# Attention scores in 64-row by 32-column tiles of the array instead of 64 by 64

## The chip, the cores and the metric

The kernel runs on one core of one Trainium2 chip. The metric is the device time of one execution in microseconds (us); the time of a kernel is the median of its runs.

## The reference

A sliding-window attention with linear position biases, followed by a two-layer block with a hard-swish in between. Batch 8, 8 heads, 576 positions, 64 numbers a head; 4608 tokens of width 512, inner width 2048.

```
scores = (1/sqrt(64)) * q @ k.T                       # per batch and head, 576 x 576
mask   = (rel >= 0) & (rel < 128)                     # rel = query position - key position
scores = where(mask, scores - slope[h] * abs(rel), -1e9)
attn   = softmax(scores)
x      = (attn @ v), heads side by side               # 4608 x 512
h      = x @ w_in
out    = (h * clip(h + 3, 0, 6) / 6) @ w_out
```

A query sees itself and the 127 keys before it. Seen from a key at place p of a block of 128 keys, the queries that can see it are those at places p to p + 127, counted from the block's start.

## The kernel before, in words

The order of the instructions on every engine is written out by hand (a manual schedule), and each engine works through its own in that order. The work is 32 groups `g`, one for each batch and pair of heads (head `e` is 0 or 1, and sits in rows 64e to 64e + 63 of the transposed queries `qT` and keys `kT`). Batches 0 and 1 have code of their own (`first_batch`, `second_batch`); from batch 2 on, `segment` takes one group after the other. In each turn it has, for group `g`: `scores` (matmuls of keys and queries), `exp_diag` and `exp_off` (exponentials on ScalarE, then a triangular mask on GpSimd), and for group `g - 1` `values` (the matmuls with v and the division) and `back` (the way into `xT`, from which the second part reads). Between these stand calls of `fill`, each of which puts one unit of the two-layer block there: four matmuls with 512 columns, by `moe_up` (L502) or `moe_down` (L552).

The scores of a group stand in two tiles `sce`, one for each head: 128 keys of a block in the partitions, and for each of four key blocks `j` 256 queries, as `s` = 0 (the queries of the same block, read by `exp_diag`) and `s` = 1 (those of the next block, read by `exp_off`). The fifth block has only 64 keys and 64 queries; its scores go into a corner of block 3 that is otherwise free (L373), read through `p4buf`. The first group with this layout, `g` = 8, is computed by `scores_whole` over whole blocks and fills both tiles; the groups after it, 9 to 31, use the loop at L359 to L374. It cuts a key block into two halves of 64 keys (`half`, first key `lo`), and for each half takes only 192 queries from `lo` on, since no other query sees any of these keys. A matmul there uses 64 rows of the array (one head's 64 numbers) and 64 columns (64 keys), a quarter of it; head and half give four such quarters. Places of `sce` that are not written keep older scores, and the masks after the exponentials (L406, L415, L421) put zeros there.

Of the kernel before, what the change touches and what calls it, by code (L numbers as in the profile page):

```python
# [18 lines left out]
def kernel(  # L19
# [9 lines left out]
    nc = tc.nc  # L29
    B, H, S, D = q.shape  # L30
# [7 lines left out]
    LAST = S - 4 * 128  # L38
# [222 lines left out]
    def full(g):  # L261
        return g < NB_FULL * NP
# [12 lines left out]
    def rooms(g):  # L275
        b, hp = divmod(g, NP)
        if full(g):
            room = w_out_sb if b == 0 else gbuf[1]
            for i, nm in enumerate(("pd", "po")):
                st[g, nm] = room[:, ds(4 * hp + 2 * i, 2), :].rearrange(  # L280
                    "p e (j c) -> p e j c", j=4)
        else:
            st[g, "pd"] = ppool.tile([128, 2, 4, 128], BF16, tag="pd", name="pd")
            st[g, "po"] = ppool.tile([128, 2, 4, 128], BF16, tag="po", name="po")

    def scores_diag(g):
        rooms(g)
        b, hp = divmod(g, NP)
        qT, kT = qTb[b % 2][:, hp, :, :], kTb[b % 2][:, hp, :, :]
        first = not diag_tabled(g)  # L290
        if (g, "scd") not in st:
            tables_diag(g)
        scd = st[g, "scd"]
        for j in range(4):
            for e in range(2):
                r = slice(e * D, (e + 1) * D)
                nc.tensor.matmul(scd[:, e, ts(j, 128)], lhsT=kT[r, j, :],
                                 rhs=qT[r, j, :], start=first, stop=first or j == 3)
# [15 lines left out]
    def scores_off(g):  # L314
        b, hp = divmod(g, NP)
        qT, kT = qTb[b % 2][:, hp, :, :], kTb[b % 2][:, hp, :, :]
        foff = not full(g)
        if (g, "sco") not in st:
            tables_off(g)
        sco = st[g, "sco"]  # L320
        for e in range(2):
            r = slice(e * D, (e + 1) * D)
            nc.tensor.matmul(sco[:, e, 64:128], lhsT=kT[r, 4, :],
                             rhs=qT[r, 4, 0:LAST], start=foff, stop=foff)
        for j in range(4):
            n = 128 if j < 3 else LAST
            for e in range(2):
                r = slice(e * D, (e + 1) * D)
                nc.tensor.matmul(sco[:, e, ds((j + 1) % 4 * 128, n)], lhsT=kT[r, j, :],
                                 rhs=qT[r, j + 1, 0:n], start=foff, stop=foff or j == 3)  # L330
    def scores_whole(kT, qT, sce):
        for j in range(4):
            for e in range(2):
                r = slice(e * D, (e + 1) * D)
                n = min(256, S - 128 * j)
                nc.tensor.matmul(
                    sce[e][:, j, :, :].rearrange("p s c -> p (s c)")[:, 0:n],
                    lhsT=kT[r, j, :], rhs=qT[r, ds(128 * j, n)], start=True, stop=True)
        for e in range(2):
            r = slice(e * D, (e + 1) * D)  # L340
            nc.tensor.matmul(sce[e][:, 3, 1, 64:128], lhsT=kT[r, 4, :], rhs=qT[r, 512:S],
                             start=True, stop=True)

    def scores(g):
        if full(g):
            scores_diag(g)
            scores_off(g)
            return
        rooms(g)
        b, hp = divmod(g, NP)  # L350
        qT = qTb[b % 2][:, hp, :, :].rearrange("p j c -> p (j c)")
        kT = kTb[b % 2][:, hp, :, :]
        if g == 2 * NP:
            st["sce"] = [ps_sc.tile([128, 4, 2, 128], FP32, tag="sc", name="sce")
                         for _ in range(2)]
            scores_whole(kT, qT, st["sce"])
            return
        sce = st["sce"]
        for j in range(4):  # L359
            for half in range(2):  # L360
                lo = 64 * half
                n = min(192, S - 128 * j - lo)
                for e in range(2):
                    r = slice(e * D, (e + 1) * D)
                    nc.tensor.matmul(  # L365
                        sce[e][lo:lo + 64, j, :, :].rearrange("p s c -> p (s c)")[:, ds(lo, n)],
                        lhsT=kT[r, j, lo:lo + 64], rhs=qT[r, ds(128 * j + lo, n)],
                        start=True, stop=True)
        for half in range(2):
            lo = 64 * half  # L370
            for e in range(2):
                r = slice(e * D, (e + 1) * D)
                nc.tensor.matmul(sce[e][lo:lo + 64, 3, 1, 64:128], lhsT=kT[r, 4, lo:lo + 64],  # L373
                                 rhs=qT[r, 512:S], start=True, stop=True)  # L374

    def exp_off_full(g):
        nc.scalar.activation(out=st[g, "po"].rearrange("p e j c -> p e (j c)"),  # L377
# [290 lines left out]
    def second_batch():  # L668
# [12 lines left out]
        for i in range(4):  # L681
            load_w_out(i)
        g = 2 * NP - 1
        scores(g)
        exp_diag(g, 0)
        exp_diag(g, 1)
# [25 lines left out]
        done[0] = 2 * NP  # L712
        fill(2)
        scores(2 * NP)

    FILLS = {g: (1, 1, 1, 2, 0, 1, 1) for g in (9, 10, 11, 13, 14, 15)}

    def segment(lo, hi, fills):
        for g in range(lo, hi + 1):
# [3 lines left out]
            if lo < g < hi and g != 3 * NP + 1:  # L723
                scores(g)
# [88 lines left out]
```

## Time and profile before

| | before |
|---|---|
| time, median of 3 runs (lowest, highest) | 322.15 us (321.69, 322.75) |
| span of the profiled execution | 319.2 us |
| busy time of TensorE / weight loads | 310.1 / 164.9 us |
| busy time of ScalarE, VectorE, GpSimd | 195.7, 173.1, 141.2 us |
| score matmuls with 192 or 128 columns (L365) | 368, busy 11.9 us |
| score matmuls of the fifth block (L373) | 92 |

The time of a run covers a little more than the span, which goes from the first to the last instruction of the program. PE is TensorE, PEld its weight loads, ACT ScalarE, DVE VectorE, POOL GpSimd. "64*64 64x192" in a row is the tile of the array that a matmul uses, and then partitions by columns of what it reads. Matmuls run one into the other: the duration that the profile gives to one holds its way through the array, so that the distance from start to start tells what it costs in a series, and a busy TensorE may still be waiting in part.

### The profile page before, as it was taken

To read this page: it belongs to the slowest core of one execution; us is meant where nothing else is said; L and a number is where in the kernel's file an instruction comes from. 1 tells how busy PE (TensorE), PEld (TensorE's weight loads), DVE (VectorE), ACT (ScalarE), POOL (GpSimd) and SP (SyncE) were. 2 spreads that over 40 slices of the span, in tenths; PEclk is the share of its full clock that TensorE was granted. 3 is DMA by queue.
4 is the path that set the end of the run, shared out by engine and by line. 5 is a ranking of instruction groups with operands and counts; after the bars stand their busy time and mean duration, and the time that the engine had idled before them with its cause. 6 is when DMAs were issued, how large, how long until landed. Compare 5 with 4: busy or idle time off the path is not lost.

```text
span 319.2 us, 7124 instructions
## 1 busy us (share of the span) xinstructions
PE 310.1 (97%) x2775; PEld 164.9 (52%) x2775; DVE 173.1 (54%) x338; ACT 195.7 (61%) x334; POOL 141.2 (44%) x249
## 2 busy tenths in 40 slices
PE   7879999999999999999999999999999999999996
PEld 5565465455545454445677654444444444444443
DVE  6667675554355655655565556555656455455510
ACT  4748976877767776676676667666764344244401
POOL 8464493684496477266744673663331000000000
PEclk9999999999999999999999999999999999999999
DMA  7999999999999999998999999962212110000112
GB/s 281 199 323 225 256 260 195 249 231 194 215 252 157 239 208 211 205 222 194 207 205 211 209 190 196 225 93 68 38 39 88 53 36 33 33 33 35 66 56 75
DMA packets 131425, 51.90 MB, mean 163 GB/s; under 512 B 118976, under 2 KB 123328, under 8 KB 131392
## 3 DMA queue, kind: packets, MB, share of 16 engines
q1 hardware_dynamic: 126160, 45.36, 68.0%
q0 software_dynamic: 4224, 4.19, 8.2%
q10 hardware_dynamic: 1008, 1.90, 1.6%
q8 instruction: 21, 0.34, 0.5%
q14 instruction: 12, 0.10, 0.1%
HBM read 36.70 MB, written 9.44 MB: 145 GB/s over the span
## 4 chain that ended last, share of the span: by engine, by line
PE 86%; DMA 5%; ACT 4%; POOL 2%; DVE 2%; issue 1%; POOLq 0%
PE ops L552 38%; PE hps L502 36%; DMA w_in_sb<-in_moe_w_in_dram 3%; PE sce L365 3%; PE av L442 2%; PE av L434 2%; DMA ldbuf<-in_k_dram 2%; ACT r L521 2%; PE ops L533 1%; ACT kTb L245 1%; ACT gbuf L399 1%; PE tp L243 1%; DVE gbuf L522 0%; ACT gbuf L377 0%; PE tb L483 0%
## 5 line engine op out<-in xcount | busy, mean ns | idle before, releaser
L522 DVE SCALAR_TENSOR_TENSOR gbuf<-r,hps 128x512 bf16<-128x512 f32 x144 | 98.7, 688 | 101.0 <-ACT r L521 99.8
L521 ACT ACTIVATE r<-hps,bias 128x512 f32<-128x512 f32 x144 | 98.9, 689 | 86.8 <-PE hps L502 86.6
L502 PE MATMUL hps<-xT,w_in_sb 128*128 128x512 bf16 (+1 forms) x640 | 144.9, 358 | 0.6 <-ACT xT L489 0.3
L552 PE MATMUL ops<-w_out_sb,gbuf 128*128 128x512 bf16 x560 | 137.8, 379 | 0.0
L502 PEld LDWEIGHTS <-w_in_sb 128*128 128x128 bf16 x640 | 59.3, 98 | 55.0 <-issue 0.8
L552 PEld LDWEIGHTS <-gbuf 128*128 128x128 bf16 x560 | 51.9, 98 | 56.3
L415 POOL TENSOR_SCALAR_AFFINE_SELECT po<-po 128x512 bf16<-128x512 bf16 x48 | 30.3, 636 | 32.5 <-ACT po L413 32.4
L406 POOL TENSOR_SCALAR_AFFINE_SELECT pd<-pd 128x512 bf16<-128x512 bf16 x48 | 29.8, 634 | 33.5 <-ACT pd L389 33.5
L389 ACT ACTIVATE pd<-sce,bias_d 128x512 bf16<-128x512 f32 x48 | 31.7, 684 | 5.4 <-PE sce L373 2.7
L561 DVE COPY osb<-ops 128x512 f32<-128x512 f32 x33 | 22.7, 688 | 20.0 <-PE ops L552 17.5
L195 POOL CAST tbuf<-ldbuf 128x512 bf16<-128x512 f32 (+1 forms) x45 | 25.6, 614 | 16.8 <-issue 9.3
L413 ACT ACTIVATE po<-sce,bias_o 128x512 bf16<-128x512 f32 x48 | 33.0, 687 | 0.0
L453 DVE TENSOR_TENSOR avs<-av,rc 128x384 bf16<-128x384 f32 (+1 forms) x48 | 23.6, 491 | 1.6
L442 PEld LDWEIGHTS <-pd 128*128 128x128 bf16 x192 | 14.3, 97 | 8.3 <-issue 0.5
L434 PE MATMUL av<-vbuf,po 128*128 128x65 bf16 x192 | 18.0, 193 | 0.0
L442 PE MATMUL av<-vbuf,pd 128*128 128x65 bf16 x192 | 17.3, 193 | 0.3 <-ACT kTb L245 0.3
L434 PEld LDWEIGHTS <-po 128*128 128x128 bf16 x192 | 14.3, 98 | 2.9 <-DVE avs L453 0.5
L188 POOL CAST vbuf<-ldbuf 128x1024 bf16<-128x1024 f32 x14 | 14.2, 1043 | 3.5 <-DMA ldbuf<-in_v_dram 3.5
L418 ACT ACTIVATE p4buf<-sce,bias_d 128x64 bf16<-128x64 f32 x48 | 15.5, 323 | 0.0
L228 POOL CAST pr<-ldbuf 128x576 bf16<-128x576 f32 x20 | 12.9, 670 | 5.1 <-DMA ldbuf<-in_k_dram 3.1
L365 PE MATMUL sce<-qTb,kTb 64*64 64x192 bf16 (+1 forms) x368 | 11.9, 245 | 0.0
L365 PEld LDWEIGHTS <-kTb 64*64 64x64 bf16 x368 | 7.1, 106 | 8.6 <-issue 8.5
(104 smaller groups left out, 208.4 us busy)
## 6 DMA issues: line engine op xcount, KB each, us to landing
out_dram<-osb SPq DMA_DIRECT2D x33, 256.0 KB, 2.5
ldbuf<-in_v_dram SPq DMA_DIRECT2D x32, 256.0 KB, 5.2
ldbuf<-in_q_dram SPq DMA_DIRECT2D x20, 256.0 KB, 5.3
ldbuf<-in_k_dram SPq DMA_DIRECT2D x16, 256.0 KB, 4.4
ldbuf<-in_q_dram SPq DMA_DIRECT2D x12, 288.0 KB, 7.0
ldbuf<-in_k_dram SPq DMA_DIRECT2D x12, 288.0 KB, 6.3
w_in_sb<-in_moe_w_in_dram POOLq DMA_DIRECT2D x4, 512.0 KB, 9.2
w_out_sb<-in_moe_w_out_dram POOLq DMA_DIRECT2D x4, 512.0 KB, 10.3
```

The source lines that it names most:

```text
L195: nc.gpsimd.tensor_copy(out=tbuf[:m, :, j, :], in_=s[:m, j, :, :].rearrange("p (i e) d -> p i (e d)", e=2))
L365: nc.tensor.matmul(sce[e][lo:lo + 64, j, :, :].rearrange("p s c -> p (s c)")[:, ds(lo, n)], lhsT=kT[r, j, lo:lo + 64], rhs=qT[r, ds(128 * ...
L389: nc.scalar.activation(out=pd[:, e, :, :], in_=st["sce"][e][:, :, 0, :], func=ACT.Exp, bias=bias_d[:, h:h + 1], scale=scale)
L406: nc.gpsimd.affine_select(out=pd[:, e, :, :], in_=pd[:, e, :, :], pattern=[[0, 4], [1, 128]], channel_multiplier=-1, base=0, compare_op=AL ...
L413: nc.scalar.activation(out=po[:, e, :, :], in_=sc[:, :, 1, :], func=ACT.Exp, bias=bias_o[:, h:h + 1], scale=scale)
L415: nc.gpsimd.affine_select(out=po[:, e, :, :], in_=po[:, e, :, :], pattern=[[0, 4], [-1, 128]], channel_multiplier=1, base=-1, compare_op=A ...
L434: nc.tensor.matmul(out_av, lhsT=po[:, e, qt % 4 if full(g) else qt - 1, :], rhs=vb[:, qt - 1, h, :], start=True, stop=False)
L442: nc.tensor.matmul(out_av, lhsT=d, rhs=vb[:, qt, h, :], start=(qt == 0), stop=True)
L502: nc.tensor.matmul(hps[:, lo:hi], lhsT=w_in_sb[:, ks, ts(ms, 128)], rhs=xT[:, ks, ds(src, hi - lo)], start=(ks == 0), stop=(ks == n_ks - 1))
L521: nc.scalar.activation(out=r6, in_=hps, func=ACT.Relu, bias=bias3[:, 0:1], scale=1.0 / 6.0)
L522: nc.vector.scalar_tensor_tensor(out=gts[nt][:, ms, :], in0=r6, scalar=1.0, in1=hps, op0=ALU.min, op1=ALU.mult)
L552: nc.tensor.matmul(ops[nt, sub], lhsT=gts[nt][:, ms, ts(sub, 128)], rhs=w_out_sb[:, ms, :], start=(ms == 0), stop=(ms == n_ms - 1))
```

## The change

The loop over halves becomes a loop over eighths of the array: each key block is cut into four groups of 32 keys, and each group takes 160 queries from its first key on. In the fifth block, two groups of 32 keys cover the 64 keys (before, two halves of 64 rows covered these and 64 rows of padding), and each takes the queries from its first key on. Sizes of `sce`, the exponentials, the masks and everything else stay.

```
         for j in range(4):
-            for half in range(2):
-                lo = 64 * half
-                n = min(192, S - 128 * j - lo)
+            for lo in range(0, 128, 32):
+                n = min(160, S - 128 * j - lo)
                 for e in range(2):
                     r = slice(e * D, (e + 1) * D)
                     nc.tensor.matmul(
-                        sce[e][lo:lo + 64, j, :, :].rearrange("p s c -> p (s c)")[:, ds(lo, n)],
-                        lhsT=kT[r, j, lo:lo + 64], rhs=qT[r, ds(128 * j + lo, n)],
+                        sce[e][lo:lo + 32, j, :, :].rearrange("p s c -> p (s c)")[:, ds(lo, n)],
+                        lhsT=kT[r, j, lo:lo + 32], rhs=qT[r, ds(128 * j + lo, n)],
                         start=True, stop=True)
-        for half in range(2):
-            lo = 64 * half
+        for lo in range(0, LAST, 32):
             for e in range(2):
                 r = slice(e * D, (e + 1) * D)
-                nc.tensor.matmul(sce[e][lo:lo + 64, 3, 1, 64:128], lhsT=kT[r, 4, lo:lo + 64],
-                                 rhs=qT[r, 512:S], start=True, stop=True)
+                nc.tensor.matmul(sce[e][lo:lo + 32, 3, 1, 64 + lo:128],
+                                 lhsT=kT[r, 4, lo:lo + 32], rhs=qT[r, 512 + lo:S],
+                                 start=True, stop=True)
```

## The prediction, made before the changed kernel ran

> **What bounds the kernel now.** I read the page first (busy shares and the chain of waits), then the stretches by stage, then who waited for whom while the changed code runs, then the timeline of one score section with its rows by line.
>
> ```profile
> PE 310.1 (97%) x2775; PEld 164.9 (52%) x2775; DVE 173.1 (54%) x338; ACT 195.7 (61%) x334; POOL 141.2 (44%) x249
> ...
> PE 86%; DMA 5%; ACT 4%; POOL 2%; DVE 2%; issue 1%; POOLq 0%
> PE ops L552 38%; PE hps L502 36%; DMA w_in_sb<-in_moe_w_in_dram 3%; PE sce L365 3%; PE av L442 2%; PE av L434 2%; DMA ldbuf<-in_k_dram 2%; ACT r L521 2%; PE ops L533 1%; ACT kTb L245 1%; ACT gbuf L399 1%; PE tp L243 1%; DVE gbuf L522 0%; ACT gbuf L377 0%; PE tb L483 0%
> ```
>
> TensorE is busy 97% of the span and carries 86% of the chain; the score matmuls of the changed loop (line 365) are themselves 3% of it. No other engine is over 61%. The stretches by stage show whether TensorE ever waits where the changed code stands:
>
> ```profile
> 61.00:89.00 28.00, 27.64 (x275) 14.50 (x275) 14.05 (x29) 21.13 (x40) 18.03 (x31) 1.00 1.08 221
> 89.00:105.00 16.00, 15.77 (x148) 8.08 (x149) 9.20 (x19) 11.49 (x21) 13.16 (x24) 1.00 1.11 208
> 105.00:145.00 40.00, 40.00 (x368) 19.89 (x366) 23.19 (x46) 27.38 (x51) 23.20 (x41) 1.00 1.13 212
> 145.00:185.00 40.00, 40.00 (x410) 25.85 (x402) 22.77 (x45) 26.78 (x50) 23.78 (x43) 1.00 1.10 209
> 185.00:234.00 49.00, 49.00 (x443) 24.50 (x443) 27.40 (x55) 32.59 (x60) 23.84 (x43) 1.00 0.69 130
> ```
>
> The columns are length, then busy time of PE, PEld, DVE, ACT and POOL, granted clock, DMA share and GB/s. From 105 to 234 us TensorE is busy all of the time at the full granted clock (1.00); before that it has 0.36 + 0.23 = 0.59 us of idle time. The changed lines run only in this part:
>
> ```profile
> L365 PEld LDWEIGHTS <-kTb x368: 102/106/107, 61.1 to 233.4; 64*64 64x64 bf16 x184
> L365 PE MATMUL sce<-qTb,kTb x368: 216/243/267, 61.1 to 233.5; 64*64 64x192 bf16 x161, 64*64 64x128 bf16 x23
> L373 PE MATMUL sce<-qTb,kTb x92: 189/189/189, 61.5 to 233.5; 64*64 64x64 bf16 x92
> ```
>
> There are 368 / 16 = 23 sections, from 61.1 to 233.5 us. Whatever a section gets shorter or longer moves everything behind it on an engine that is always busy, so the question is only how long one section is. Here is one, with the big matmuls around it. The rows between the first and the last are the same matmuls asked for in later and later narrow stretches, so that the count shows how many have started:
>
> ```profile
> 112.19 0.38 PE L502 MATMUL hps<-xT,w_in_sb 128*128 128x512 bf16 x1
> 112.50 0.28 PE L365 MATMUL sce<-qTb,kTb 64*64 64x192 bf16 x4
> 112.50 0.36 PE L365 MATMUL sce<-qTb,kTb 64*64 64x192 bf16 x8
> 112.50 0.44 PE L365 MATMUL sce<-qTb,kTb 64*64 64x192 bf16 x12
> 112.50 0.52 PE L365 MATMUL sce<-qTb,kTb 64*64 64x192 bf16 x16
> 112.83 0.21 PE L373 MATMUL sce<-qTb,kTb 64*64 64x64 bf16 x4
> 112.97 1.04 PE L552 MATMUL ops<-w_out_sb,gbuf 128*128 128x512 bf16 x4
> 113.85 1.03 PE L502 MATMUL hps<-xT,w_in_sb 128*128 128x512 bf16 x4
> ```
>
> Three things are to be seen. The matmuls come in waves of four (two heads by two halves of the keys), one wave for each of the four key blocks: the union grows 0.28, 0.36, 0.44, 0.52, that is 0.08 us a wave. Within a wave the four run beside each other: the first wave's union is 0.28 with single matmuls of 0.267, so all four started within some 13 ns. And the section costs 0.47 us from its first start (112.50) to the next big matmul (112.97); big matmuls follow each other every (113.85 - 112.97) / 4 = 0.22 us, and the section starts 0.31 us after the last one, so 0.09 us more goes in draining before it. At its end the last narrow matmul starts at 112.83 + 0.21 - 0.19 = 112.85.
>
> **What a column costs.** The durations 189, 216 and 243 ns belong to 64, 128 and 192 columns: 27 ns for 64, 0.42 ns a column. So 192 columns are 81 ns, which is the 0.08 us of a wave: a wave is as long as one tile's stream of columns, not as long as its instructions. The last matmul's 64 columns end at 112.85 + 0.03 = 112.88, and 0.09 us of draining follow, as at the start.
>
> **The change part by part.** *Columns.* Of the four 32-key groups the first has the most to stream: 160 + 160 + 160 + 160 + 64 = 704 columns, where the first half now has 4 x 192 + 64 = 832. The other three groups have 672, 608 and 576. If eight tiles run beside each other as four do now, the path is 128 columns shorter: 128 x 0.42 = 54 ns a section.
>
> *First weight load.* The first wave's matmuls show 267 ns where later ones show 243: 24 ns in which they wait for their 64 columns of weights. With 32 columns I take half, 12 ns saved; the bounds are 0 (a fixed price) and 24.
>
> *Starting eight instead of four.* 13 ns for four starts makes about 27 ns for eight. The last group to start is the one with 576 columns, 54 ns less than the first, so the later start is hidden; without that cover it would cost 14 ns.
>
> *More instructions.* The built program has 36 pairs of weight load and matmul in a section instead of 20, so 736 more instructions on TensorE, in 23 places; the two draining stretches stay at two a section, since both lines still share one tile shape. The order of all else, on all engines, is unchanged, and no instruction gains or loses a wait, so nothing new is queued behind anything. A wave of 160 columns (67 ns) must be fed 16 instructions, 4.2 ns each, against 8 in 81 ns now. The longest run of small pairs in the trace is this one:
>
> ```profile
> 5.25 0.76 PE L220 MATMUL tp<-ident,pr 64*64 64x64 bf16 x36
> L220 PE MATMUL tp<-ident,pr x144: 192/193/213, 5.3 to 13.7; 64*64 64x64 bf16 x144
> ```
>
> 36 pairs start within 0.76 - 0.19 = 0.57 us, 16 ns a pair. There, though, only two tiles are in use and 64 columns last 27 ns, so 36 pairs need 18 x 27 = 0.49 us for their columns alone; the row bounds the supply from one side only. From the other side, four pairs start in 13 ns. I take the supply as sufficient, since pairs pile up behind 0.22 us matmuls ahead of most sections, but this is a bound that the trace does not close.
>
> *Masks and the last block.* The last block now writes only 32-key rows that hold keys and only queries from the group's first on. What is left out is replaced by the triangular masks on GpSimd, which stay; ACT's and GpSimd's instructions keep their sizes. No cost, no gain.
>
> **The sum.** 54 + 12 = 66 ns a section, 23 sections: 1.52 us. Five sections begin before 91 us, where TensorE has its 0.59 us of idle time, so up to 5 x 66 = 0.33 us may turn into waiting. With no gain in the weight load and all five swallowed it is 18 x 54 ns = 0.97 us; the ends are 0.97 and 1.52, and I take 1.35, the full sum less half of the 0.33. The profiled span of 319.2 us becomes 317.85. The runs' median, 322.15, lies 2.95 us above that span, which the change does not touch, so the forecast is 322.15 - 1.35 = 320.8 us, itself 320.6 to 321.2. About 0.3% (0.97 us) is what a measurement here can tell from no change: the gain is just above that.
>
> On eight tiles at once no row here says anything: at most four are in use. The Trainium skill, "TensorE: Matmul & The Clock Gate", section "Measured speedup vs the span model", gives sixteen 32x32 tiles with 512 columns a speedup of 10.6 and some 4 ns for each further tile; by it eight would run at once and the sum would stand. Four starts in 13 ns in this trace agree with its 4 ns; its width is shown by no run here.
>
> **Rivals.** *1. Pairs are not supplied fast enough (slower).* Place: the queue into TensorE inside each section. At the 16 ns of the row above, the 36th pair starts 35 x 16 = 0.56 us after the first, where the last now starts at 0.35: 0.21 us more a section, 4.8 us in all, 327.0 us. It decides from 0.35 / 35 = 10 ns a pair. For it: 36 pairs in about 0.3 us have no example in the trace. Against it: that row's 16 ns is mostly its columns, and line 365 already starts 16 matmuls in about 0.28 us without a gap between waves. Its full price holds only if no pairs are waiting at the section's start; with half of them waiting, the price is about halved, 324.5.
>
> The Trainium skill, "TensorEngine Tiling (Array Packing)", section "Instruction Overhead", states some 60 cycles for each matmul on this chip, which would be a rule against this change. By it, as an estimate at 25 ns each, 16 more a section would cost 16 x 25 x 23 = 9.2 us, 331.4 us. The trace disagrees for matmuls in different tiles, whose four starts took 13 ns.
>
> *2. Eight streams do not run at full rate (slower).* Two heads by four groups read four streams of queries from the same partitions, twice today's. If only four tiles advance at a time, a block takes 2 x 67 ns: the columns come to 7 x 67 + 54 + 27 = 550 ns where they are now 832 x 0.42 = 349, so 0.20 us more a section, 4.6 us, 326.8 us. It decides from (349 + 12 - 27) / 4 = 84 ns a wave of eight, 25% over the 67. For it: nothing in the trace uses a 32-column tile. Against it: two groups of columns show no slowing at all, a wave being exactly its columns.
>
> *3. The gain is swallowed (no change).* DMA shares of 1.08 to 1.13 between 61 and 185 us leave transfers little room to come earlier, and in the waits of 61 to 234 us GpSimd already has some:
>
> ```profile
> POOL tbuf L195 <- DMA qTb<-tbuf: 7.5, 2, 5.7
> ```
>
> If batches then arrive no sooner, TensorE waits for what it saves and the time is 322.15. Against it: with no idle TensorE from 105 us on and a share of 0.69 in the last stage, loads run ahead; a lead of at most 1.5 us, built up over 170, is small beside them.
>
> **Chances.** Forecast 0.61, rival 1 0.12, rival 2 0.15, rival 3 0.12. A few hundredths of the forecast's case fall under 0.97 us. So faster by over 0.3%: 0.58; within: 0.15; slower: 0.27. The range begins at 320.3 (a little under the full sum) and reaches to 324.0, into the milder forms of rivals 1 and 2; it leaves out their full prices, a little under 2 in 10. The forecast's own range is 320.6 to 321.2.
>
> **What would show it.** In the changed profile's timeline, waves of eight of the new matmuls should add 0.07 us each to the union, and a section should take about 0.41 us from its first start to the next big matmul. Waves of 0.13 us, or two groups of four starts, would be rival 2; gaps between starts within a wave, weight loads late, rival 1. A section of 0.41 with new idle time on TensorE after it, ended by DMA, would be rival 3. A section over 0.47 us makes the forecast wrong.

## The result and the profile after

| comparison | before, median us | changed, median us | ratio, 95% interval |
|---|---|---|---|
| first, 6 and 6 runs | 322.74 | 320.60 | 0.9946 [0.9927, 0.9965] |
| second, 26 and 12 runs | 322.45 | 322.93 | 1.0016 [0.9990, 1.0042] |
| third, 29 and 12 runs | 322.57 | 322.11 | 0.9988 [0.9962, 1.0014] |

The first comparison is the one that the prediction answers to: 320.60 us against a forecast of 320.8, 0.54% faster. In the second and the third, on two different chips (that of the first is not recorded), the same kernel was not measurably faster. In the second, 5 of the 12 runs of the changed kernel and 1 of the 26 of the kernel before had a mean granted clock of 0.995 or less, and without them the medians are 322.46 and 322.45 us. What the change does to one section is the same in all three profiles of the changed kernel; what becomes of it is not.

First the section. This is the eighth in the first profile of the changed kernel, asked for as before: start and length in us, then the count of matmuls that have started.

```profile
112.15 0.38 PE L501 MATMUL hps<-xT,w_in_sb 128*128 128x512 bf16 x1
112.46 0.26 PE L364 MATMUL sce<-qTb,kTb 64*32 64x160 bf16 x8
112.46 0.33 PE L364 MATMUL sce<-qTb,kTb 64*32 64x160 bf16 x16
112.46 0.40 PE L364 MATMUL sce<-qTb,kTb 64*32 64x160 bf16 x24
112.46 0.46 PE L364 MATMUL sce<-qTb,kTb 64*32 64x160 bf16 x32
112.74 0.19 PE L371 MATMUL sce<-qTb,kTb 64*32 64x64 bf16 x4
112.87 1.04 PE L551 MATMUL ops<-w_out_sb,gbuf 128*128 128x512 bf16 x4
```

Waves of eight, 0.07 us apart, and 0.41 us to the next big matmul, where it was 0.47. In unrounded starts the median section went from 479 to 412 ns, and all 23 together from 11.02 to 9.48 us: 1.55 us less TensorE time. The draining at both ends is as it was: 0.31 us ahead of the section.

Then the stretches (length, busy time of PE, PEld, DVE, ACT and POOL, clock, DMA share, GB/s):

```profile
89.00:105.00 16.00, 15.69 (x181) 8.12 (x181) 9.22 (x19) 11.50 (x22) 11.57 (x22) 1.00 1.05 227
105.00:145.00 40.00, 39.74 (x432) 19.54 (x430) 23.21 (x46) 27.11 (x50) 24.58 (x44) 1.00 1.15 203
145.00:185.00 40.00, 40.00 (x494) 26.12 (x494) 22.76 (x45) 27.05 (x50) 24.04 (x43) 1.00 1.18 212
185.00:234.00 49.00, 49.00 (x557) 24.60 (x557) 27.41 (x55) 32.59 (x60) 23.86 (x43) 1.00 0.73 136
```

From 105 to 145 us TensorE is no longer busy all of the time: 0.26 us is missing, at a place where the kernel before had none. The timeline shows what ended it:

```profile
122.88 0.81 PE L501 MATMUL hps<-xT,w_in_sb 128*128 128x512 bf16 x3
123.95 0.81 PE L501 MATMUL hps<-xT,w_in_sb 128*128 128x512 bf16 x3 [0.26 <-DMA xT<-avs]
```

This is the first up unit of a token tile. Its fourth matmul reads the part of `xT` that a DMA transpose has just written, and the transpose is late. Three matmuls at 0.22 us would have put it at 123.53; it starts at 123.95, so 0.42 us is lost (the idle time in the row is shorter, because a duration covers part of the wait). The span is 318.8 us, just 0.4 under that of the kernel before, though the sections are 1.55 us shorter. The first section also began 0.4 us later, in code that the change does not touch.

### The profile page after: what moved, and what is told of

Same layout as the page of the kernel before. It is cut to its first block, busy times and chain, and to the rows that moved or that the text cites. A ratio compares the mean times of both kernels' runs of the same rounds, so it can differ in the third digit from the quotient of the medians.

```text
span 318.8 us, 7860 instructions
## 1 busy us (share of the span) xinstructions
PE 309.7 (97%) x3143; PEld 165.3 (52%) x3143; DVE 173.2 (54%) x338; ACT 195.8 (61%) x334; POOL 140.8 (44%) x249
## 4 chain that ended last, share of the span: by engine, by line
PE 86%; ACT 5%; DMA 3%; DVE 2%; issue 1%; SPq 1%; POOL 0%; POOLq 0%; ACTq 0%
PE ops L551 37%; PE hps L501 36%; PE sce L364 2%; DMA ldbuf<-in_q_dram 2%; PE av L441 2%; ACT r L520 2%; PE av L433 2%; PE ops L532 1%; DVE gbuf L521 1%; PE w L153 1%; DMA xT<-avs 1%; PE tp L220 1%; PE tp L255 1%; ACT kTb L245 1%; SPq L98 1%
## 5 line engine op out<-in xcount | busy, mean ns | idle before, releaser
L451 DVE RECIPROCAL rc<-av 128x6 f32<-128x6 f32 (+1 forms) x48 | 8.8, 183 | 4.3 <-PE av L441 4.3
L364 PEld LDWEIGHTS <-kTb 64*32 64x32 bf16 x736 | 6.2, 91 | 8.7 <-issue 7.6
```

## The experiments

The first four runs share a chip, the next four another, the three after them a third, and the last has one of its own; each is compared with runs of the kernel before on the same chip.

**The eight tiles with the old number of columns.**

```
-                n = min(160, S - 128 * j - lo)
+                n = min(192, 256 - lo, S - 128 * j - lo)
```

> The eight 64x32 tiles stay, but the first two key groups of a block stream 192 columns again and the third 192 (the fourth keeps 160), so the first group streams 832 columns, as before the change. Theory (a section is as long as its longest column stream, plus the first weight load): a section of 0.412 + 128 x 0.42 ns = 0.466 us against 0.479 before and 0.412 after; 23 x 13 ns = 0.3 us under the kernel before, about no change. Rival (the gain comes from the smaller tiles as such, or from the fifth block): a section stays near 0.412 us and the time near that of the changed kernel, 1.5 us under before.

The median section took 465 ns, 1 from the expected 466. The row by line shows 254 ns for the first wave and 242 after it, so a weight load of 32 columns still delays the first wave by 12 ns, and the rest of the length is columns:

```profile
L364 PE MATMUL sce<-qTb,kTb x736: 202/242/254, 61.4 to 233.8; 64*32 64x192 bf16 x112, 64*32 64x160 bf16 x49, 64*32 64x96 bf16 x23
```

Ratio 1.0000 [0.9976, 1.0025]: no change, as expected. Smaller tiles as such bring 14 ns a section; the 32 columns fewer in each of the four waves bring the other 53.

**The same pairs in another order.**

```
-        for j in range(4):
-            for lo in range(0, 128, 32):
+        for half, j in [(half, j) for half in range(2) for j in range(4)]:
+            for lo in (64 * half, 64 * half + 32):
```

> The same 36 pairs of the changed kernel in another order: all four key blocks for key groups 0 and 1, then all four for groups 2 and 3, so that four tiles work at a time instead of eight. Theory (matmuls start in their order, and eight tiles at once are what makes the section short): the second half starts behind the fourth wave of the first, 12 + 3 x 69 + 10 = 229 ns, and takes 3 x 69 + 56 ns more plus 92 of draining: a section of about 0.58 us, 0.10 over before, so 2.4 us over before. Rival (each tile takes its own matmuls as soon as it is free, whatever the order): the section stays at 0.41 us and the time at that of the changed kernel.

My theory of the order fell: the median section took 423 ns, not 580. The timeline shows why:

```profile
112.70 0.25 PE L364 MATMUL sce<-qTb,kTb 64*32 64x160 bf16 x4
112.70 0.30 PE L364 MATMUL sce<-qTb,kTb 64*32 64x160 bf16 x8
112.70 0.32 PE L364 MATMUL sce<-qTb,kTb 64*32 64x160 bf16 x12
```

Four more matmuls started 53 ns after the first four, and the next four at 81 ns, a full wave after the first. The four at 53 ns can only be in the tiles that were free, those of the second half, which stand twelve pairs further back in the program; and it is in this second chain that the 128- and 96-column matmuls of the last block appear, at 272 ns. So a matmul for a free tile passes those that wait for a busy one, and the late start of the second chain costs the section only 11 ns, since its last block has fewer columns. The ratio was 0.9999 [0.9972, 1.0026]: 56 ns a section, 1.3 us in all, did not arrive in the time. That was the first hint that TensorE's savings are lost elsewhere.

**One more change of the tile shape.** The fifth block in 64x64 tiles:

```
-        for lo in range(0, LAST, 32):
-            for e in range(2):
-                r = slice(e * D, (e + 1) * D)
-                nc.tensor.matmul(sce[e][lo:lo + 32, 3, 1, 64 + lo:128],
-                                 lhsT=kT[r, 4, lo:lo + 32], rhs=qT[r, 512 + lo:S],
-                                 start=True, stop=True)
+        for e in range(2):
+            r = slice(e * D, (e + 1) * D)
+            nc.tensor.matmul(sce[e][0:64, 3, 1, 64:128],
+                             lhsT=kT[r, 4, 0:64], rhs=qT[r, 512:S],
+                             start=True, stop=True)
```

> The changed kernel, but the fifth block's scores are two matmuls in 64x64 tiles, so that the tile shape changes once more inside a section. Theory (each change of shape costs some 0.09 us of draining): 12 + 4 x 69 = 288 ns, 92 of draining, 24 + 27 ns for load and columns, 92 of draining: a section of 0.52 us, 0.04 over before, so 1.0 us over before and 2.5 us over the changed kernel. Rival (only going to and from whole-array matmuls costs draining): 0.41 us, the time of the changed kernel.

```profile
113.89 0.46 PE L364 MATMUL sce<-qTb,kTb 64*32 64x160 bf16 x32
114.28 0.22 PE L370 MATMUL sce<-qTb,kTb 64*64 64x64 bf16 x2
114.43 0.61 PE L550 MATMUL ops<-w_out_sb,gbuf 128*128 128x512 bf16 x2
```

The two matmuls start 0.39 us into the section, where the last columns of the tiles ahead end at 0.29: the change of shape costs 0.10 us, also between two small shapes. The section took 536 ns (expected 520), and the time followed: 1.0064 [1.0043, 1.0085], 2.1 us more against 23 x 57 ns = 1.3. The rest, 0.8 us, may be waits: between 100 and 240 us TensorE waits for two DMA transposes here, though its sections are longer than in the kernel before, whose profile has no such wait.

```profile
PE hps L500 <- DMA xT<-avs: 0.3, 1, 0.3
PE sce L364 <- DMA kTb<-tbuf: 0.3, 1, 0.3
```

On this chip longer sections arrive in the time in full, shorter ones do not.

**64 columns for each matmul.** Most of the scores are left out.

```
-                n = min(160, S - 128 * j - lo)
+                n = min(64, S - 128 * j - lo)
```

> The changed kernel with 64 columns for each matmul in place of 160; most of the scores are left out. It asks how fast pairs of weight load and matmul can be fed. Theory (columns set the pace): 12 + 4 x 29 + 29 + 92 = 250 ns a section, 229 ns under before, 5.3 us in all where the saving passes, less where transfers come late. Rival (the supply of pairs is near its limit): at 16 ns a pair the section would be 0.68 us, over before; at 10 ns a pair 0.47 us, as before. If the section is short but the time does not follow, transfers swallow it.

```profile
114.48 0.32 PE L364 MATMUL sce<-qTb,kTb 64*32 64x64 bf16 x32
114.71 0.21 PE L371 MATMUL sce<-qTb,kTb 64*32 64x64 bf16 x4
114.85 0.82 PE L551 MATMUL ops<-w_out_sb,gbuf 128*128 128x512 bf16 x3
```

The section took 368 ns, not 250. The 32 matmuls of line 364 start within 0.13 us (0.32 less 0.19 for the last), 4 ns a pair. The four of line 371 follow only 0.23 us after the first start, 0.10 us late, and then 8 ns apart in unrounded starts. So rival 1 seems to have a real core: 32 pairs were ready and the rest had still to be fed. That reading is not tested by itself, since no run changed the number of pairs. In the changed kernel the 32nd pair starts at 240 ns and the 33rd must wait for columns until 287 anyway, which covers it. And again the time stayed, 1.0001 [0.9978, 1.0025], with sections 2.6 us shorter in all. In its waits between 100 and 236 us TensorE has this:

```profile
PEld L364 <- DMA kTb<-tbuf: 2.0, 3, 1.1
PE hps L501 <- DMA xT<-avs: 0.8, 2, 0.5
PE sce L364 <- DMA kTb<-tbuf: 0.6, 1, 0.6
```

**Taking load off the transfers.** If late transposes take the saving, it must come back when transfers have room. Both kernels were run with two of five token blocks of q, k and v not loaded from batch 4 on (older numbers are used), next to the changed kernel as it is:

```
-        for j in range(NQ):
+        for j in range(NQ) if b < 4 else (0, 1, 4):
```

> The changed kernel once more, on the chip of the runs below. Theory (each section is 67 ns shorter, 1.54 us in all, but part of it turns into waits for DMA transposes into xT and kTb, some 0.4 to 0.7 us in one profile): 0.8 to 1.2 us under before, with waits for DMA at the first up matmul of a token tile near 123 us. Rival (all of it passes, and the waits seen in one profile were chance): 1.5 us under before and no such wait.

> The kernel before, which from batch 4 on leaves out the loading of two of the five token blocks of q, k and v (older numbers stand in their place), so that transfers have room. Theory (TensorE sets the pace of the kernel before, transfers only just keep up): sections as before, 0.479 us, and the time of before or up to 0.5 us under it, since the waits for transposes that some executions have go away. Rival (transfers set the pace already): over 1 us under before.

> The changed kernel with the same loads left out. Theory (what the change saves on TensorE is lost only to late transposes): no wait for DMA on TensorE, and the full 23 x 67 ns = 1.5 us under the kernel before with the same loads left out. Rival (TensorE's saving is lost to something else, such as the supply of instructions): about as far under as in the pair with all loads, below 1.2 us.

| same chip | median us | ratio to before |
|---|---|---|
| changed kernel | 322.93 | 1.0016 [0.9990, 1.0042] |
| before, fewer loads | 321.98 | 1.0000 [0.9978, 1.0021] |
| changed, fewer loads | 320.27 | 0.9939 [0.9912, 0.9967] |

The changed kernel with all loads was expected 0.8 to 1.2 us under before and was no faster. With fewer loads the two kernels lie 1.71 us apart, with all loads they lie together. The kernel before gains nothing from fewer loads. In the stretches of the changed kernel with fewer loads the DMA share is down, and TensorE is busy throughout:

```profile
105.00:145.00 40.00, 40.00 (x466) 19.95 (x464) 23.26 (x47) 27.61 (x52) 23.45 (x42) 1.00 0.99 173
145.00:185.00 40.00, 40.00 (x495) 26.13 (x494) 22.79 (x45) 26.50 (x50) 24.11 (x43) 1.00 0.67 138
185.00:234.00 49.00, 49.00 (x523) 24.40 (x522) 27.38 (x54) 32.85 (x61) 23.22 (x41) 1.00 0.55 110
```

With all loads, on the same chip, the timeline has these waits (0.58 and 0.34 us of idle time; 0.81 and 0.51 us by the starts):

```profile
126.51 0.81 PE L501 MATMUL hps<-xT,w_in_sb 128*128 128x512 bf16 x3 [0.58 <-DMA xT<-avs]
190.92 0.81 PE L501 MATMUL hps<-xT,w_in_sb 128*128 128x512 bf16 x3 [0.34 <-DMA xT<-avs]
```

The first and the last start of the score matmuls, in the rows by line, say the same for the whole attention. These are the changed kernel in its first and second profile, the kernel before with fewer loads, and the changed kernel with fewer loads:

```profile
L364 PE MATMUL sce<-qTb,kTb x736: 202/229/241, 61.5 to 233.1; 64*32 64x160 bf16 x161, 64*32 64x128 bf16 x23
L364 PE MATMUL sce<-qTb,kTb x736: 202/229/241, 63.6 to 235.9; 64*32 64x160 bf16 x161, 64*32 64x128 bf16 x23
L365 PE MATMUL sce<-qTb,kTb x368: 216/243/267, 62.2 to 234.5; 64*64 64x192 bf16 x161, 64*64 64x128 bf16 x23
L364 PE MATMUL sce<-qTb,kTb x736: 202/229/241, 61.5 to 232.5; 64*32 64x160 bf16 x161, 64*32 64x128 bf16 x23
```

The kernel before took 172.4 us from one to the other, 172.3 with fewer loads. Twenty-two sections 67 ns shorter make 1.5 us, so 170.9 if all of it passes. The changed kernel took 171.6 in its first profile (half passed), 172.3 in its second (next to nothing), and 171.0 with fewer loads (nearly all). That settles what I could settle: the saving is there each time, and late transposes take a part of it, here half and nearly all, that differs from one execution to the next. (In the second profile the granted clock was 0.83 from 20 to 30 us, where the first has 1.00, and the first section starts 2.1 us later than there, ahead of anything changed.)

Why are the transposes late? SyncE issues the loads, the transposes and most of the stores one after the other (SPq; the second number is how long the issue took). These are the issues of the transpose that the first up unit near 123 us needs, in the kernel before and in the changed kernel's first profile, its second, and its third, which belongs to a comparison below:

```profile
120.00 1.23 SPq L476 DMA_TRANSPOSE xT<-avs  x1
120.79 1.61 SPq L475 DMA_TRANSPOSE xT<-avs  x1
123.21 1.24 SPq L475 DMA_TRANSPOSE xT<-avs  x1
120.98 1.59 SPq L475 DMA_TRANSPOSE xT<-avs  x1
```

The row of up matmuls that needs it starts 3.1 us after the issue in the kernel before (at 123.06), and 2.1, 1.8 and 1.7 us after it in the changed kernel (at 122.88, 125.05 and 122.68). The nine sections ahead of that place save 0.6 us, so the rest is a later issue. From 100 to 121 us that queue issues without a pause of more than 0.1 us in the kernel before and in the changed one; with fewer loads it has pauses of over 1 us in both. Whether the queue or the DMA engines behind it set the pace, no run separates, since fewer loads relieve both.

The later issue does not come from shorter sections alone. From the first score section to the issue of the transpose of q near 95 us it is 33.7 us in the kernel before (94.8 - 61.1) and 34.0 in its variant with the later need of `xT`, tried below, and it is 34.2 to 36.0 us in the ten profiles with small tiles and all loads, among them the run with 192 columns (35.4), which saves next to nothing, and the one with longer sections (36.0). Why the transfers of the kernels with small tiles run later, no run shows. One candidate is the code itself: the pages of the kernel before and of the changed kernel show 21 and 24 packets of instructions fetched by DMA:

```profile
q8 instruction: 21, 0.34, 0.5%
q8 instruction: 24, 0.39, 0.6%
```

**Three tries at giving the transposes room.** None made a version that beats both kernels.

*More down units first, and the loads of v behind the transposes of k* (the code for the loads is not shown):

```
-             ("DDDD", "UUDUDUDUD", "UUDUDUDUD", "UUDUDUDDUU"),
+             ("DDDDD", "UUDUDUDUD", "UUDUDUDUD", "UUDUDUDUU"),
```

> The changed kernel with more room for the transposes: five down units instead of four before the first up unit of each later token tile (one less near its end), so that the first matmul that reads a new part of xT comes 0.86 us later, and the loads of v from batch 4 on issued behind the transposes of k instead of ahead of them. Theory: the wait near 123 us and the waits for kTb shrink or go; 0.3 to 0.6 us under the changed kernel. Rival (the waits only move to other transfers): the same time as the changed kernel.

3.65% slower [3.19%, 4.11%]. Down units come in fours that share one PSUM bank, and a fifth in a row waits until VectorE has emptied it. The waits of TensorE over the span show it 14 times:

```profile
PE ops L551 <- DVE osb L560: 7.0, 14, 0.8
```

These are 7.0 of the 12.2 us that the kernel is over before. So this says nothing on the transposes; the edit brought a wait of its own. The loads of v behind the transposes were changed with it and are not judged either.

*The fourth matmul of the first up units later:*

```
+            if fn is moe_up and step == 0 and nt > 2 and nt * NT % RING + NT <= RING:
+                up_begin(nt, 0, 3)
+                up_begin(nt, 1, 3)
```

> The changed kernel beside the kernel before a third time, as the measure for the two runs below. The first comparison had it 0.54% faster, the second no faster. Theory (sections 67 ns shorter everywhere; how much of it waits for transposes differs from execution to execution and chip to chip): between 0 and 1.7 us under before, and the waits for xT in the profile make up the difference to 1.5 us. Rival (the change brings nothing at all, the first comparison was chance): within 0.3 us of before.

> The changed kernel, in which five of the later token tiles begin with the first three of the four matmuls of two up units before the fourth of each, so that the first matmul that needs the newest part of xT comes 0.65 us later with no work added. Theory (late transposes into xT take most of what the change saves): the waits for xT near 123 and 190 us go, and the time is 0.4 to 0.9 us under the changed kernel, 1.2 to 1.6 us under before where the changed kernel gains half. Rival (the loss is elsewhere, in the start of the program for example): the same time as the changed kernel.

> The same later need of xT in the kernel before. Theory (the kernel before waits little for xT, none in its profile): the same time as before, within 0.4 us. Rival (the kernel before loses as much to late transposes as the changed one): 0.4 to 0.9 us under before, and the difference between the two versions with room is again under 1 us.

The third profile of the changed kernel shows the waits at their clearest, at the first up unit near 123 us:

```profile
122.68 0.59 PE L501 MATMUL hps<-xT,w_in_sb 128*128 128x512 bf16 x2
123.54 0.38 PE L501 MATMUL hps<-xT,w_in_sb 128*128 128x512 bf16 x1 [0.26 <-DMA xT<-avs]
124.70 0.59 PE L501 MATMUL hps<-xT,w_in_sb 128*128 128x512 bf16 x2 [0.79 <-DMA xT<-avs]
```

By the starts 0.43 and 0.95 us are lost there, 1.4 in all, next to the 1.5 that the sections save; from the first to the last start of the score matmuls it took 172.6 us, so nothing passed in this execution.

On this chip the changed kernel was at 0.9988, the changed kernel with the edit at 1.0014 [0.9991, 1.0037], the kernel before with it at 1.0060 [1.0037, 1.0083]. Both expectations of the edit itself were wrong: it needs two PSUM banks at once, and waits for VectorE to free the second, five times:

```profile
PE hps L501 <- DVE gbuf L521: 1.4, 5, 0.4
```

But it does what it was meant for: no wait for `xT` is left on TensorE. And with it the two kernels lie 1.95 us apart (322.85 and 324.80), as the pair with fewer loads did. The wait that the edit brings is the same in both profiles (1.4 us, five times). By the medians the edit costs the kernel before 2.2 us and the changed kernel only 0.7, and the difference, 1.5 us, is what the sections save.

*Every unit one place later, without cost:*

```
-    FILLS = {g: (1, 1, 1, 2, 0, 1, 1) for g in (9, 10, 11, 13, 14, 15)}
+    FILLS = {g: (1, 1, 1, 2, 0, 1, 1) for g in (9, 10, 11, 12, 13, 14, 15)}
```

> The changed kernel with one unit of the two-layer block fewer in the turn of group 12 (7 instead of 8, as in the turns around it), so that from there on every unit stands one place later against the attention's steps and the first up unit of each token tile comes 0.86 us later against the transposes into xT, with no work, no bank and no wait added. Theory (late transposes into xT take what the change saves): no wait for xT on TensorE between 100 and 235 us, and 1.2 to 1.6 us under before. Rival (the waits move to kTb or the loss is elsewhere): within 0.8 us of before, as the changed kernel was in its second and third comparison.

0.9989 [0.9965, 1.0013]: the rival. The waits for `xT` are gone, and others stand in their place (TensorE, 100 to 236 us):

```profile
PEld L433 <- POOL po L414: 1.0, 2, 0.5
PE av L433 <- POOL po L414: 0.7, 2, 0.4
PE sce L364 <- DMA kTb<-tbuf: 0.5, 1, 0.5
PE av L441 <- POOL pd L405: 0.4, 1, 0.4
```

GpSimd's masks stand behind its casts into `tbuf`, which wait for the transposes of q, now 11.0 us of waiting against 7.5 in the kernel before. The longer wait ends at 135.6 us, and TensorE waits for the masks at 139.7 to 140.9:

```profile
POOL tbuf L195 <- DMA qTb<-tbuf: 11.0, 2, 7.2
```

So it seems that the limit is not one late transfer but the transfers of the stretch as a whole: here one reader was given room, and others were next.

## Why the prediction was right, and where it was not

- **A wave is its columns; eight tiles at once.** Right: 128 columns at 0.42 ns were to save 54 ns, and the first experiment puts them at 53. Waves of eight run at full rate (0.07 us a wave), so rival 2 fell. The Trainium skill ("TensorE: Matmul & The Clock Gate", "Measured speedup vs the span model") has sixteen tiles at once; the rows here agree for eight, with starts some 3 ns apart. By the Trainium skill's same page, section "The mechanism", matmuls start strictly in program order; the second experiment shows otherwise, with four that passed twelve others, and there the measurement decides.
- **First weight load.** Right: half of 24 ns; 12 are left.
- **Supply of pairs.** Right in the kernel, with less to spare than I thought: the 64-column kernel shows a gap of 0.10 us after 32 pairs, which the changed kernel's columns hide. The 60 cycles a matmul that the Trainium skill states ("TensorEngine Tiling (Array Packing)", "Instruction Overhead") are not paid one after another by matmuls in different tiles: 32 starts in 0.13 us.
- **The section.** 66 ns forecast, 67 measured, 1.5 us in all.
- **What of it reaches the time.** This is the step that failed. I bounded the loss by TensorE's 0.59 us of old idle time (0.33 us lost at most), and held against rival 3 that TensorE never waited from 105 us on. The three profiles lost about half, nearly all and all of the 1.5 us. No wait is not the same as room. In the profile of before, the transpose that was late afterwards is issued at 120.0 us and takes 3.1 us to land, and the matmul that needs it is the fourth of a row that starts at 123.06:

```profile
123.06 1.67 PE L502 MATMUL hps<-xT,w_in_sb 128*128 128x512 bf16 x7
L476 SPq DMA_TRANSPOSE xT<-avs x1: 1232/1232/1232, 120.0 to 120.0; - x1
DMA to landing us min/median/max: 3.1/3.1/3.1
```

  The fourth starts at 123.06 + 3 x 0.22 = 123.7, so the transpose had landed 0.6 us before: no more than the nine sections ahead of it save. With DMA shares of 1.1 that was the row to weigh, and rival 3 deserved several times its 0.12. I also held that nothing new is queued behind anything. But the transposes were issued later against TensorE's work, by more than the shorter sections explain.
- **What lies outside the span.** I took the 2.95 us between the span of before and its median as untouched by the change. That was not so. In all 111 runs of the changed kernel and its variants whose spans are on record, 1.66 to 1.78 us lie outside the span. Of 101 runs of the kernel before on four chips, 30 have over 1.9 us, up to 3.08. In the first comparison it was 1.73 us in the profiled run of the changed kernel (320.53 - 318.8). In that of the kernel before it was at least 2.49 (321.69 - 319.2), whichever of the three runs was the profiled one.
- **The number.** The forecast of 320.8 came true in the first comparison, partly by luck. The gain there was 2.1 us by the medians and 1.7 by the ratio, where 1.35 was forecast and the sections save 1.55; and the two profiles differ by only 0.4 us in span. In the two later comparisons the forecast did not come true.

What stays open: what lies outside the span in the kernel before, and so how much of the first comparison's gain comes from there; why its six runs seem to have all of the saving, though the one of them that was profiled shows half; and why the transposes are issued later.

## What to carry to other kernels

In these runs matmuls in separate tiles of the array cost the longest column stream of any one tile, so with narrower tiles a band of scores pays only for the columns that its keys need, as long as the pairs are ready. An engine that never waits has not been shown to have room behind it: before counting a saving on it, measure for each transfer it reads how long before its use it lands (0.6 us here), and where that is no more than the saving up to there, expect to lose part of it. Check afterwards whether the transfers are still issued when they were. To see where a saving went, lighten the suspect in both kernels and compare the pair.

## What the runs showed of the hardware that I had not expected

- A matmul whose tile is free starts ahead of earlier ones whose tiles are busy: 53 ns into the section instead of behind twelve other pairs.
- After 32 pairs of weight load and matmul in 0.13 us the next came 0.10 us late, and then every 8 ns.
- A change between two small tile shapes costs as much as one to or from the whole array does: 0.10 us against 0.09.
